# Hardware loops for half of the weighted sums over V in a two-problem decode attention kernel

## The chip, the cores and the metric

The kernel runs on one core of a Trainium2 chip. A core has TensorE (PE: matrix products, with a separate queue PEld for loading the stationary operand), VectorE (DVE), ScalarE (ACT), GpSimd (POOL) and SyncE (SP), and 16 DMA engines that bring data from HBM into the on-chip memory. The metric is the device time of one execution in microseconds (us), the median of three runs. Lower is better.

## What is computed

Two independent problems, A and B, of the same shape are solved one after the other and their results are put side by side. Each is one decoding step of attention with a sliding window: two sequences, one query position, 32 query heads that share 16 key/value heads, a head size of 128, and the last 4096 of 16384 cached positions.

```python
W = min(4096, max(256, Sk // 4))                       # 4096
q = (x @ wq) ...                                       # 2 x 32 heads x 128
k, v = k_cache[:, :, Sk - W:, :], v_cache[:, :, Sk - W:, :]   # each shared by 2 query heads
p = softmax(q k^T * Dh ** -0.5)
o = p v
return o @ wo                                          # 2 x 1 x 576 per problem
```

Each key and value is used by two query heads only, so there is little arithmetic per byte: the caches alone are 134 MB, and the profile counts 153 MB read from HBM.

## The kernel before, in words

**Slabs.** The work is cut into 16 slabs, eight per problem: slab i belongs to group G = i // 2 (four key/value heads) and to sequence b = i % 2. A slab has one K part and one V part of 4 MB each. Both go through a ring of four buffers (`ring`, 32,768 bytes per partition each). SP issues all large transfers, in the order in which the list `stream` has them (K of slab t, then V of slab t - 3, with parts of the output weights `wob` after every four slabs), and waits before each until the last reader of the ring buffer has finished (line 373). The last reader of a K part is the second DVE transposition `X` (line 436), the last reader of a V part is the last matmul of `PV` (line 539).

**One step of the main loop** (lines 700 to 740) handles slab t. DVE transposes the first half of K (`X`, L436, 4.43 us each), PE multiplies it with the queries (`S`, 16 matmuls, recorded at L462 and, through a helper that reuses loaded weights, at L266), then the same for the second half. Between them stand DVE's evacuation of the sum over V from the step before (`evac`, L562 and L569) and, in turn, the maximum of a group (L470) or the turning of its probabilities (`pT`, L509). After the second half, PE does a small transposition (`bias`, L490) or sums (`sums`, L520, and `dg`, L576), and then the sum over V of slab t - 3.

**The sum over V** (`PV`, `pv_moving`, L528) has eight rounds of four matmuls. Each matmul takes 32 columns of the turned probabilities `pT` as stationary operand and 512 columns of the V part as moving operand; the four of a round use the four 32-column strips of the PE array and accumulate into four strips of the PSUM bank `OTB`. Every matmul brings its own weight load. All are written out: 32 matmuls and 32 loads per slab, 512 of each in all.

**P in memory.** `pT` holds, for each of two groups in turn, 2048 columns as [h][b][j][q] with h the half of K, b the sequence, j 64 positions and q eight rows, so that the columns of one sequence are two separate stretches.

**Order.** There is no scheduler: each engine runs its instructions in the order of the calls. A recorder (`_Sched`) derives the semaphore waits, and `emit` (L813) writes the streams out: SP, PE, DVE, ACT, POOL.

**The end.** After the last V part come the last pieces of the output weights of problem B (cut in lines 162 and 360), the products with them (`proj`), two evacuations to `out_w` and the output transfers (L694).

Of the kernel before, what the change touches and what calls it, by code (L numbers as in the profile page):

```python
# [63 lines left out]
def build_kernel(nc, probs, out):  # L64
# [17 lines left out]
    KJ = W // 32  # L82
    SW = KJ * 128
# [3 lines left out]
    NSLAB = NG * Bb  # L87
# [6 lines left out]
    with es:  # L94
        sb = lambda name, shape, dt: es.enter_context(nc.sbuf_tensor(name, shape, dt))
        ring = sb("ring", [128, NSLOT, SW], BF16)
# [3 lines left out]
        pR = sb("pR", [128, 2048], BF16)  # L100
        pT = sb("pT", [128, 2, 2048], BF16)
# [38 lines left out]
        OTB = ps("ot")  # L140
# [6 lines left out]
        ringf = ring[:].rearrange("p r f -> p (r f)")  # L147
# [32 lines left out]
        for P in range(NPROB):  # L180
            def f_wq(e, P=P):
# [7 lines left out]
        pe = lambda fn, deps, tag: S.add("pe", fn, deps, tag)  # L189
# [3 lines left out]
                                                   base=0, channel_multiplier=1), [p_ones_f], "ident_f")  # L193
        p_ones_b = pool(lambda e: e.memset(ones_b[:], 1.0), [], "ones_b")
        p_ident_b = pool(lambda e: e.affine_select(ident_b[:], ones_b[:], [[-1, 128]], ALU.is_equal, 0.0,
                                                   base=0, channel_multiplier=1), [p_ones_b], "ident_b")
# [126 lines left out]
        for t in range(NSLAB + LAG):  # L323
            if t < NSLAB:
                stream.append(("K", t))
            if t >= LAG:
                i = t - LAG
# [178 lines left out]
        def make_pT(G):  # L506
            v = G % 2
            deps = [exp_op[G]] + ([PVop[2 * (G - 2) + 1]] if G >= 2 else [qt_op])
            pT_op[G] = dve(lambda e: e.transpose(  # L509
                pT[:, v, :].rearrange("p (w j q) -> p j w q", w=4, q=8),  # L510
                pR[:].rearrange("p (j w q) -> p j w q", w=4, q=8)), deps, "pT%d" % G)

        def make_rsum(G):
            ch[(G, "rsum8")] = pool(lambda e: e.tensor_tensor(
# [13 lines left out]
        def pv_moving(i, j0, j1):  # L528
            G, b = i // 2, i % 2
            v = G % 2  # L530
            r = slot_of[("V", i)]

            def f(e):
                for rd in range(j0 // 16, j1 // 16):
                    jh, j = rd // 4, 16 * (rd % 4)
                    base = (2 * jh + b) * 512 + 8 * j
                    for c in range(4):
                        jj = 16 * rd + 4 * c
                        last = e.matmul(OTB[32 * c:32 * c + 32, :], pT[:, v, base + 32 * c:base + 32 * c + 32],  # L539
                                        ring[:, r, jj * 128:(jj + 4) * 128], start=rd == 0, stop=rd == KJ // 16 - 1, skip_group_check=True)  # L540
                return last
            return f

        def make_PV(i, ks=None):
            ensure(("V", i))
            G, b = i // 2, i % 2
            parts = stream_dma[("V", i)]
            for c0, c1, dma in parts if ks is None else [parts[k] for k in ks]:
                deps = [dma, pT_op[G], evac_op[i - 1] if i >= 1 else q_ev[0]]
                PVop[i] = pe(pv_moving(i, c0, c1), deps, "PV%d_%d" % (i, c0))  # L550
            last_reader[("V", i)] = PVop[i]
# [148 lines left out]
        for t in range(NSLAB):  # L700
            i = t - LAG
# [13 lines left out]
            if Gs is not None:  # L715
                make_rsum(Gs)
                make_pT(Gs)
# [23 lines left out]
        i = T - LAG  # L741
# [9 lines left out]
        make_pick(NG - 2)  # L751
        make_rsum(NG - 1)
        make_pT(NG - 1)
        make_sums(NG - 1)
        make_PV(i + 2)
# [57 lines left out]
        def emit(eng_name, engine):  # L813
            for op in S.ops[eng_name]:
                for s_h, val in waits_of[id(op)]:
                    engine.wait_ge(s_h, val)
                last = op.fn(engine)
                if op.shared is not None:
                    last.then_inc(op.shared, 1)
                elif op.dma is None:  # L820
                    last.then_inc(ev[eng_name], 1)

        emit("sp", nc.sync)
        nc.sync.wait_ge(out_sem, dma_count[out_sem])
        emit("pe", nc.tensor)
        emit("dve", nc.vector)
        emit("act", nc.scalar)
        emit("pool", nc.gpsimd)


def bass_concat_heads__sliding_block_cached__sliding_block_cached__decode_kernel(
    nc, A_x, A_k_cache, A_v_cache, A_wq, A_wo, B_x, B_k_cache, B_v_cache, B_wq, B_wo, out,
):
    build_kernel(nc, [(A_x, A_k_cache, A_v_cache, A_wq, A_wo), (B_x, B_k_cache, B_v_cache, B_wq, B_wo)], out)
# [28 lines left out]
```

## Time and profile before

| what | value |
|---|---|
| time, median of 3 runs (lowest to highest) | 363.1 us (363.03 to 363.24) |
| time of the profiled execution | 363.1 us |
| its span, first to last instruction | 361.8 us |
| mean granted TensorE clock | 0.887 |
| data read from HBM | 153.1 MB, 423 GB/s over the span |
| busy: PE, DVE, ACT, POOL | 63%, 60%, 13%, 7% |
| PE instructions recorded | 1357 matmuls, 943 weight loads |
| sums over V (L539) | 512 matmuls, 32.0 us busy; 512 loads, 12.4 us busy |

The page of the profile has numbered parts: busy time by engine, the span in 40 slices, the DMA queues, the chain of work that ended last, the costliest groups of instructions (busy us, mean ns of one, idle time before them and what ended it), and the DMA issues. Other views are the timeline of a stretch, the busy time in chosen windows, one source line with its instructions, and who waited for whom. `SPq`, `PEldq` and the like are the engines' sequencers. `q8 instruction` is a DMA queue that brings instructions.

### The profile page before, as it was taken

The page shows a single profiled execution, that of the slowest core. Times are in us where ns is not written, and L with a number is a line of the kernel's source. Part 1 is how long each engine was busy: PE and PEld are TensorE (multiplying, and loading weights), DVE is VectorE, ACT ScalarE, POOL GpSimd, SP SyncE. Part 2 cuts the span into 40 slices and gives each one's busy share as a digit, 9 for nine tenths or more (in the row PEclk, how much of TensorE's full clock was granted, in tenths as well). Part 3 has the DMA queues.
Part 4 walks back from the last instruction along what each step waited for, and adds up shares of the span by engine and source line. Part 5 has one row for each costly group of instructions (what it writes and reads, how often), then busy time and mean ns, then how long its engine had stood idle before and what let it go on. Part 6 is the DMA issues. An engine that isn't in the chain of part 4 may idle for free.

```text
span 361.8 us, 2701 instructions
## 1 busy us (share of the span) xinstructions
PE 229.0 (63%) x1357; PEld 56.1 (16%) x943; DVE 218.6 (60%) x150; ACT 45.4 (13%) x77; POOL 24.3 (7%) x84
## 2 busy tenths in 40 slices
PE   0397687767464866671696656662776675667575
PEld 0010111112110211120121211110112121112222
DVE  0811898495949392924919493952927776675522
ACT  1002100040031002200005000500005000500500
POOL 4200101100010001000010000000010000001000
PEclk9999698969999889888798998899589897869989
DMA  8999999999999999999999999999999999999996
GB/s 327 449 428 420 442 426 424 446 413 446 417 447 420 442 422 422 439 438 420 438 424 434 431 438 412 448 420 442 424 435 429 428 438 420 434 442 420 427 417 258
DMA packets 6088, 153.28 MB, mean 424 GB/s; under 512 B 684, under 2 KB 828, under 8 KB 1084
## 3 DMA queue, kind: packets, MB, share of 16 engines
q1 hardware_dynamic: 6056, 153.10, 98.7%
q8 instruction: 9, 0.15, 0.2%
q14 instruction: 3, 0.02, 0.0%
q10 hardware_dynamic: 20, 0.01, 0.0%
HBM read 153.10 MB, written 0.00 MB: 423 GB/s over the span
## 4 chain that ended last, share of the span: by engine, by line
DMA 49%; DVE 24%; PE 16%; issue 8%; ACT 1%; POOL 1%; SPq 0%
DMA ring<-in_B_k_cache_dram 25%; DVE xt L436 15%; DMA ring<-in_B_v_cache_dram 9%; DMA ring<-in_B_wq_dram 7%; DMA ring<-in_A_k_cache_dram 6%; PE st L266 6%; PE st L462 5%; DMA wob<-in_B_wo_dram 3%; DVE oR L569 2%; DVE mx L470 2%; DVE pT L509 2%; PE pj L266 2%; DVE tmp L562 2%; PE ot L539 1%; ACT pR L500 1%
## 5 line engine op out<-in xcount | busy, mean ns | idle before, releaser
L462 PE MATMUL st<-xt,zq 128*128 128x512 bf16 x256 | 119.3, 466 | 93.6 <-DVE xt L436 93.6
L436 DVE STREAM_TRANSPOSE xt<-ring 128x4096 f32<-128x4096 f32 x32 | 141.6, 4429 | 33.5 <-DMA ring<-in_A_k_cache_dram 18.2
L266 PE MATMUL st<-xt,zq 128*128 128x512 bf16 x256 | 118.0, 461 | 0.0
L500 ACT ACTIVATE pR<-st,bias 128x512 bf16<-128x512 f32 x32 | 40.0, 1419 | 219.0 <-DVE bias L493 219.0
L462 PEld LDWEIGHTS st<-xt,zq 128*128 128x128 bf16 x256 | 28.3, 110 | 211.5 <-DVE xt L436 110.0
L539 PE MATMUL ot<-ring,pT 128*32 128x512 bf16 x512 | 32.0, 393 | 8.3 <-DMA ring<-in_B_v_cache_dram 8.3
L493 DVE SCALAR_TENSOR_TENSOR bias<-vmask,tb,offm 128x4 f32<-128x4 f32 x8 | 1.8, 224 | 37.1 <-PE tb L490 37.1
L523 DVE TENSOR_REDUCE ssum<-tb 128x2 f32<-128x8 f32 x8 | 1.3, 162 | 33.4 <-PE tb L520 33.4
L428 POOL TENSOR_TENSOR zq<-qs,bmask 128x64 bf16<-128x64 bf16 x32 | 8.6, 292 | 161.2 <-PE st L266 140.3
L509 DVE STREAM_TRANSPOSE pT<-pR 128x2048 bf16<-128x2048 bf16 x8 | 18.4, 2303 | 0.7 <-ACT pR L500 0.7
L562 DVE SCALAR_TENSOR_TENSOR tmp<-ot,rsb,dmask 128x512 f32<-128x512 f32 x16 | 11.5, 719 | 9.4 <-PE ot L539 9.4
L281 PE MATMUL ot<-ring,pT 128*32 128x512 bf16 x18 | 7.6, 421 | 15.1 <-DMA ring<-in_A_wq_dram 14.5
L539 PEld LDWEIGHTS ot<-ring,pT 128*32 128x32 bf16 x512 | 12.4, 99 | 23.7 <-DMA ring<-in_B_v_cache_dram 10.5
L569 DVE TENSOR_REDUCE oR<-tmp 128x128 f32<-128x512 f32 x15 | 15.6, 1039 | 0.5
L266 PE MATMUL pj<-ring,pT 128*32 128x512 bf16 x36 | 12.1, 422 | 0.0
L266 PE MATMUL pj<-wob,oM 128*2 128x288 bf16 (+1 forms) x64 | 10.2, 256 | 0.0
L470 DVE TENSOR_REDUCE mx<-st 128x2 f32<-128x1024 f32 x8 | 9.7, 1208 | 0.1
L500 ACT ACTIVATION_READ_ACCUMULATOR pR<-st,bias 128x1 f32 x32 | 9.1, 283 | 0.0
L636 PE MATMUL pj<-wob,oM 128*2 128x288 bf16 x32 | 7.9, 286 | 0.0
L224 DVE TENSOR_TENSOR xt<-xt,hmask 4x1152 bf16<-4x1152 bf16 x2 | 2.8, 1398 | 8.4 <-DMA xt<-in_A_x_dram 8.4
L266 PE MATMUL st<-ring,pT 128*32 128x512 bf16 x18 | 7.4, 414 | 0.0
L472 POOL TENSOR_TENSOR mv<-mx,v 128x2 f32<-128x2 f32 x8 | 1.6, 195 | 80.0 <-DVE mx L470 80.0
(71 smaller groups left out, 79.5 us busy)
## 6 DMA issues: line engine op xcount, KB each, us to landing
ring<-in_A_k_cache_dram SPq DMA_DIRECT2D x8, 4096.0 KB, 24.9
ring<-in_A_v_cache_dram SPq DMA_DIRECT2D x8, 4096.0 KB, 30.0
ring<-in_B_k_cache_dram SPq DMA_DIRECT2D x8, 4096.0 KB, 28.5
ring<-in_B_v_cache_dram SPq DMA_DIRECT2D x7, 4096.0 KB, 31.8
ring<-in_A_wq_dram SPq DMA_DIRECT2D x1, 4608.0 KB, 13.6
ring<-in_B_wq_dram SPq DMA_DIRECT2D x1, 4608.0 KB, 24.1
wob<-in_A_wo_dram SPq DMA_DIRECT2D x2, 2304.0 KB, 29.8
ring<-in_B_v_cache_dram SPq DMA_DIRECT2D x1, 2560.0 KB, 26.9
```

Source lines behind the costliest of these rows:

```text
L266: return e.add_instruction(mybir.InstMatmult(name=nc.get_next_instruction_name(), engine=mybir.EngineType.PE, ins=[e.lower_ap(mv_), e.lowe ...
L281: last = e.matmul(QB[c], wt, mv_, start=first, stop=True, skip_group_check=True)
L428: last = e.tensor_tensor(dst, src, msk, ALU.mult)
L436: Xop[(t, jh)] = dve(lambda e: e.transpose(xt[:, jh, :].bitcast(FP32).rearrange("p (kp x kt) -> p x kp kt", kp=2, kt=2), ring[:, r, jh * H ...
L462: last = e.matmul(ob, wt, mv_, start=first, stop=True, skip_group_check=True)
L470: ch[(G, "max")] = dve(lambda e: e.tensor_reduce(mx[:], st[:, :].rearrange("p (x t) -> p t x", t=2), AX.X, ALU.max), [Sop[(2 * G + 1, 1)]] ...
L500: last = e.activation(pR[:].rearrange("p (x k) -> p k x", k=4)[:, kv, :], st[:, :].rearrange("p (x t) -> p t x", t=2)[:, kv % 2, :], ACTF.Exp,
L509: pT_op[G] = dve(lambda e: e.transpose(pT[:, v, :].rearrange("p (w j q) -> p j w q", w=4, q=8), pR[:].rearrange("p (j w q) -> p j w q", w= ...
L539: last = e.matmul(OTB[32 * c:32 * c + 32, :], pT[:, v, base + 32 * c:base + 32 * c + 32], ring[:, r, jj * 128:(jj + 4) * 128], start=rd == ...
L562: evac_op[i] = dve(lambda e: e.scalar_tensor_tensor(tv, o, rsb[:, v, b:b + 1], dm, ALU.mult, ALU.mult), deps, "ev%d" % i)
L569: ch[(G, "red%d" % b)] = dve(lambda e: e.tensor_reduce(oR[:, b, :], tmp[:].rearrange("p (j d) -> p d j", j=4), AX.X, ALU.add), [evac_op[i] ...
L636: last = e.matmul(PJ[0], oM[:, j, :], mv_, start=start and j == 0, stop=True, skip_group_check=True)
```

## The change

For the eight slabs of problem A (`i < NSLAB // 2`) the rounds 1 to 6 of the sum over V become a loop of the PE sequencer, `e.Fori(1, 7)`, between a written-out round 0 and a written-out round 7. In the loop the addresses of the probabilities and of the V part come from registers: each round runs the loop body of four matmuls with their loads, five instructions that compute addresses in registers (26 register operations together), one addition to the counter and one compare-and-branch. The slabs of problem B stay written out. Matmuls executed are the same; 160 matmuls with their 160 loads leave the PE program text, and 72 register, branch and counter instructions come in.

So that one address step serves all eight rounds, `pT` is now ordered [b][h][j][q]: the columns of a sequence are one stretch of 1024. The DVE transposition that writes it gets one more dimension in its output pattern; its size stays 128 x 2048. PE's stream is now written out last, since a loop splits the program into stretches.

```diff
             pT_op[G] = dve(lambda e: e.transpose(
-                pT[:, v, :].rearrange("p (w j q) -> p j w q", w=4, q=8),
-                pR[:].rearrange("p (j w q) -> p j w q", w=4, q=8)), deps, "pT%d" % G)
+                pT[:, v, :].rearrange("p (b h j q) -> p j h b q", b=2, h=2, q=8),
+                pR[:].rearrange("p (j h b q) -> p j h b q", b=2, h=2, q=8)), deps, "pT%d" % G)
...
+            def one(e, wt_at, mv_at, first):
+                for c in range(4):
+                    wt, mv_ = pT[:, v, bass.ds(wt_at + 32 * c, 32)], ringf[:, bass.ds(mv_at + 512 * c, 512)]
+                    last = e.add_instruction(mybir.InstMatmult(
+                        name=nc.get_next_instruction_name(), engine=mybir.EngineType.PE,
+                        ins=[e.lower_ap(mv_), e.lower_ap(wt, for_matmul_weights=True)], outs=[e.lower_ap(OTB[32 * c:32 * c + 32, :])],
+                        start_tensor_calc=first, stop_tensor_calc=True, bass_skip_group_check=True,
+                        tile_size=(128, 32), tile_position=(0, 32 * c)))
+                return last
+
             def f(e):
+                if i < NSLAB // 2:
+                    one(e, b * 1024, r * SW, True)
+                    with e.Fori(1, 7) as rd:
+                        one(e, rd * 128 + b * 1024, rd * 2048 + r * SW, False)
+                    return one(e, b * 1024 + 7 * 128, r * SW + 7 * 2048, False)
                 for rd in range(j0 // 16, j1 // 16):
-                    jh, j = rd // 4, 16 * (rd % 4)
-                    base = (2 * jh + b) * 512 + 8 * j
-                    for c in range(4):
-                        jj = 16 * rd + 4 * c
-                        last = e.matmul(OTB[32 * c:32 * c + 32, :], pT[:, v, base + 32 * c:base + 32 * c + 32],
-                                        ring[:, r, jj * 128:(jj + 4) * 128], start=rd == 0, stop=rd == KJ // 16 - 1, skip_group_check=True)
+                    last = one(e, b * 1024 + rd * 128, r * SW + rd * 2048, rd == 0)
                 return last
...
         emit("sp", nc.sync)
         nc.sync.wait_ge(out_sem, dma_count[out_sem])
-        emit("pe", nc.tensor)
         emit("dve", nc.vector)
         emit("act", nc.scalar)
         emit("pool", nc.gpsimd)
+        emit("pe", nc.tensor)
```

## The prediction, made before the result was known

> **What bounds the kernel now.** I read the slices and the DMA queues first, then the chain that ended last, then the timeline of two steps in problem A, then how far SP's issues run ahead, and last the instruction queue.
>
> Page, parts 2 to 5 (slices of 9.0 us; queues as packets, MB, share of 16 engines; chain; two groups):
>
> ```profile
> PEclk9999698969999889888798998899589897869989
> DMA  8999999999999999999999999999999999999996
> ...
> q1 hardware_dynamic: 6056, 153.10, 98.7%
> q8 instruction: 9, 0.15, 0.2%
> ...
> DMA 49%; DVE 24%; PE 16%; issue 8%; ACT 1%; POOL 1%; SPq 0%
> ...
> L539 PE MATMUL ot<-ring,pT 128*32 128x512 bf16 x512 | 32.0, 393 | 8.3 <-DMA ring<-in_B_v_cache_dram 8.3
> L509 DVE STREAM_TRANSPOSE pT<-pR 128x2048 bf16<-128x2048 bf16 x8 | 18.4, 2303 | 0.7 <-ACT pR L500 0.7
> ```
>
> The DMA engines are full from start to end: data packets alone take 98.7% of all sixteen. So the kernel ends when 153 MB have come in, plus a short tail. The last step of the chain in order of time says the same:
>
> ```profile
> 348.51 10.90 DMA wob<-in_B_wo_dram
> ```
>
> From 348.51 + 10.90 = 359.41 us to the end of the span are 2.4 us of products and output, which this change does not touch. PE's work in problem A counts only if it lets the DMA queue run dry.
>
> Timeline of two steps (start, us, engine, line; in brackets the idle time before):
>
> ```profile
> 104.70 1.91 PE L539 MATMUL ot<-ring,pT 128*32 128x512 bf16 x32
> ...
> 106.66 0.54 SPq L380 DMA_DIRECT2D ring<-in_A_v_cache_dram  x1
> ...
> 109.45 0.41 PE L462 MATMUL st<-xt,zq 128*128 128x512 bf16 x1 [2.84 <-DVE xt L436]
> ...
> 124.20 1.91 PE L539 MATMUL ot<-ring,pT 128*32 128x512 bf16 x32
> ...
> 128.23 0.41 PE L462 MATMUL st<-xt,zq 128*128 128x512 bf16 x1 [2.12 <-DVE xt L436]
> ```
>
> A sum over V takes 1.91 us for 64 instructions, 30 ns each. After it PE idles 2.84 or 2.12 us until DVE has turned the next K half. SP, which waits for the last of these matmuls, issues the next transfer at once; queued behind that wait are all later transfers.
>
> **How much lateness the queue takes.** The source line of the ring transfers gives, from issue to landing:
>
> ```profile
> DMA to landing us min/median/max: 19.9/30.3/34.1
> ```
>
> 4.19 MB at 430 GB/s take 9.75 us, so an issue comes at least 19.9 - 9.75 = 10.1 us before the queue would be dry. Beside that, the compute round is shorter than the DMA round: the first X of slabs 4 and 6 start at 87.65 and 123.73, so two steps take 36.1 us; the DMA needs 4 x 9.75 for them plus 2.7 for its share of `wob` (2304 KB, 5.5 us every four slabs), 41.7 us. Spare per two slabs: 5.6 us.
>
> **The change part by part.**
>
> *The six looped rounds.* Let a round cost the sequencer r. Rows: PE's sequencer takes 51 ns for a semaphore instruction (the twelve at L816: 51/51/51); a tensor instruction passes in 30 ns. Lower bound: seven control instructions (five address steps, addition, branch) at 51 ns and eight tensor instructions at 30 ns, 0.60 us. Upper bound: the longest sequencer row, SP's 535 ns per DMA issue, for each of the seven, 3.99 us. The five address steps hold 26 register operations; if each operation costs one 51 ns row, 28 x 51 + 240 ns = 1.7 us. I take 1.7, since that row is of the same sequencer. Dispatch of the loop is then 10.2 us per slab, against 6 x 0.24 = 1.43 us of execution.
>
> Whether this shows depends on how far the sequencer runs ahead of PE. The instruction queue tells. Its nine packets of 16 KB for 2300 recorded instructions are 64 bytes each, 256 instructions per packet. The windows (PE and PEld busy, counts in brackets) ended at the second and the seventh packet:
>
> ```profile
> 0.00:108.30 108.30, 68.15 (x310) 13.23 (x176) 64.21 (x39) 12.96 (x24) 12.57 (x41) 0.92 0.99 423
> ...
> 0.00:308.65 308.65, 195.09 (x1006) 44.81 (x683) 190.94 (x118) 35.15 (x60) 23.00 (x79) 0.89 1.00 428
> ```
>
> 486 and 1689 instructions had started, 26 and 103 short of 2 x 256 and 7 x 256. If packets are fetched as the sequencer crosses a page, its lead over PE varies by 77 instructions and so reaches at least that many in places: more than the 64 of a whole sum over V. Then the loop is dispatched while PE still works on, or waits for, the K products before it: from 92.14 (first K matmul of the step) to 104.70 are 12.6 us, in the next step 109.45 to 124.20, 14.7 us; both exceed 10.2. Total dispatch per step, 10.2 plus some 76 written instructions at 30 ns, is 12.5 us of 18 to 21. So PV should start and end where it did: cost 0. Without this cover the sum would grow by e = 10.2 - 1.43 = 8.8 us per slab; that is a rival.
>
> A jump back needs its page of instructions still there; every page so far was brought once (nine packets for nine pages), and no row shows a return. [...]
>
> *pT.* Its output pattern gains a dimension. The K transposition already writes one with as many and takes 4429 ns for 4096 elements, 1.08 ns each, against 1.12 for pT: 2.2 us if it goes at that rate, 4.6 if writes halve. I take the 2.3 of now; even 4.6 adds 2.3 per two slabs, inside the spare 5.6. It has no gain to give, because DVE is not the bound.
>
> *The shorter program.* 320 instructions go, 72 come: 248, one packet of 256. A packet holds its DMA engine for 1.10 us (2.3% of 16 engines in the 3 us from 53 to 56). Nine on one engine would need 0.987 x 361.8 + 9.9 = 367 us, more than the span, so they are spread. Gain: 0 if other engines end as late, 1.1 if the one relieved was alone last. Seven or eight packets stay on others, so nearly 0; spread over sixteen, 0.07 us, which I take.
>
> *Problem B and the order of writing.* Same instructions at the same 97 ns per load and 379 ns per matmul; only the columns differ. The other engines' streams keep their order; the loops cut the program into 17 stretches, and if every stream passes a mark per new stretch, SP pays 16 x 17 ns (its semaphore row) = 0.3 us at the end, PE's 51 ns row would make it 0.8. I take 0.
>
> Sum: the profiled execution (363.1 us, span 361.8, 1.3 around it; it equals the median) + 0 - 0.07 + 0 + 0 = 363.0 us.
>
> **The rivals.**
>
> *Sequencer too slow (slower).* PV grows by e, of which 2.84 + 2.12 per two slabs is idle PE and 5.6 is spare. Lateness after four pairs is 4 x (2e - 4.96 - 5.6) = 8e - 42.2; past 10.1 us the queue runs dry, so it decides from e = 6.5. Without run-ahead e = 8.8: 28 - 10 = 18 us, 381 us. For it: no row shows a loop or a register address on PE, and a branch may empty what was queued. Against: the lead worked out above. With run-ahead it needs 6r + 2.3 above the mean 20.8 us of a step, r above 3.1.
>
> *A loop across a page (slower).* If one loop lies across two 16 KB pages and each jump back brings a page again, five returns wait for a fetch each: 1.10 us plus, say, two data packets ahead of it, 1.2 us each (in the 3 us from 53 to 56, 52 packets take 92.4% of 48 us, and 16 of them are tiny): 3.5 us, 17.5 in all, once. 2.8 are idle PE, 10.1 the least lead of the queue, so up to 4.7 us of dry queue; none at the median lead of 20.5. The further packets put a second 1.10 us on some engines. Price 1.1 to 5.8; nearer the median lead, 1.5: 364.5 us. For it: eight loops and eight page ends. Against: a body has 15 of 256 instructions, so a given loop straddles with 6%, one of eight with some 40%, and the neighbouring page may still be there.
>
> *The relieved engine was the last (faster).* -1.1 us, 362.0. Against: at least seven packets remain, each on some engine.
>
> **How the numbers follow.** No change 0.60. Sequencer 0.12, page 0.10, marks and other small costs over the bound 0.06: slower 0.28. Faster 0.12. Within 0.2% is 0.7 us, about what a measurement of this kernel can tell from no change. The range 362.2 to 366.0 takes in most of the faster rival's gain and most of the page rival; it leaves out the sequencer rival (0.12), the top of the page rival and the edge of the faster one, less than 0.2 together.
>
> **What would show it.** Right: q1 still near 98.7%; q8 with eight packets; L536 (the sums) in problem A again about 1.9 us from first to last; the K matmuls after them waiting for DVE, not for "issue"; issue to landing still near 30 us; pT at 2.3 us. Wrong: PE waiting for "issue" inside the sums, transfers landing less than 10 us after issue, DMA slices below 9, or more than nine packets on q8.

## The result, and the profile after

| | before | after |
|---|---|---|
| time, median (lowest to highest) | 363.11 us, 6 runs (363.03 to 363.34) | 364.95 us, 6 runs (363.56 to 371.78) |
| profiled execution: time, span | 363.1, 361.8 us | 363.56, 362.3 us |
| mean granted clock of it | 0.887 | 0.892 |
| ratio after / before | | 1.0045, 95% interval 1.0034 to 1.0056 |

The change costs 0.3 to 0.6%, where I forecast none. Four of its sixteen runs, one here and three in its second series, took 370.0 to 372.2 us at a granted clock of 0.866 to 0.875 and are not in the ratios, while no run of the kernel before took more than 363.5 us. The profiled execution is the quickest of the six, so the trace shows less of the loss than the median; the change was run and profiled a second time (span 363.7 us) to have a slower one.

Page of the kernel after, parts 2 to 5, the rows that answer those shown of before:

```profile
PEclk9999699969999698997989879898889888789969
DMA  8999999999999999999999999999999999999995
...
q1 hardware_dynamic: 6056, 153.10, 98.5%
q8 instruction: 8, 0.13, 0.1%
...
DVE 40%; PE 39%; DMA 9%; issue 7%; ACT 3%; POOL 1%; SPq 0%; DVEq 0%
...
L536 PE MATMUL ot<-ring,pT 128*32 128x512 bf16 (+1 forms) x512 | 57.4, 398 | 11.1 <-issue 9.3
L509 DVE STREAM_TRANSPOSE pT<-pR 128x2048 bf16<-128x2048 bf16 x8 | 18.4, 2302 | 1.2 <-ACT pR L500 1.2
```

The DMA engines are as full as before, one instruction packet fewer comes, and `pT` costs what it did. What changed is the chain that ended last: DMA had 49% of it and has 9%, DVE and PE now make up 79%. The sums over V went from 32.0 to 57.4 us busy, and PE now waits for "issue" in them.

Timeline of the sum over V in one step after (the kernel before has one row of 1.91 us there), from the matmul ahead of it to the K product behind it:

```profile
103.60 0.22 PE L490 MATMUL tb<-ident_f,nMrep 1*128 1x1 f32 x1 [1.28 <-POOL nMrep L486]
103.75 1.04 PE L536 MATMUL ot<-ring,pT 128*32 128x512 bf16 x8
105.05 0.88 PE L536 MATMUL ot<-ring,pT 128*32 x4 [0.26 <-issue]
106.19 0.85 PE L536 MATMUL ot<-ring,pT 128*32 x4 [0.26 <-issue]
107.32 0.85 PE L536 MATMUL ot<-ring,pT 128*32 x4 [0.28 <-issue]
108.43 0.89 PE L536 MATMUL ot<-ring,pT 128*32 x4 [0.26 <-issue]
109.58 1.15 PE L536 MATMUL ot<-ring,pT 128*32 x8 [0.26 <-issue]
110.66 0.41 PE L462 MATMUL st<-xt,zq 128*128 128x512 bf16 x1
```

Each looped round takes 1.13 us (105.05, 106.19, 107.32, 108.43) where a written one takes 0.24. The whole sum takes 6.9 us (103.75 to 110.66) where it took 1.91: e = 5.0 us. From first to last matmul six of the eight looped sums take 6.4 to 7.2 us, those of slabs 0 and 5 4.2 and 4.8. The K product behind it, which waited 2 to 3 us for DVE before, now starts without a wait.

PE's sequencer, by source line (count, then duration in ns, minimum/median/maximum): the address steps, the counter's instructions and the branch.

```profile
L538 PEldq FUSED_REGOPS  x192: 42/74/79, 82.6 to 243.3; - x192
...
L546 PEldq FUSED_REGOPS  x48: 78/78/83, 82.5 to 242.7; - x48
L546 PEldq ALU_OP  x48: 36/36/42, 83.5 to 243.5; - x48
L546 PEldq COMPARE_BRANCH  x48: 83/220/353, 83.6 to 243.6; - x48
```

A round is four address steps at 74, one at 78, the addition at 36 and the branch at 220 ns, 0.63 us; eight tensor instructions at 30 ns make 0.87; the 0.26 left stand in no row. Of the 48 branches, those that jump back measure 215 to 353 ns (median 220), and the last of each loop 83.

The lead of the transfers over the queue, by the source line of the ring transfers, after:

```profile
DMA to landing us min/median/max: 16.6/22.6/33.3
```

It was 19.9/30.3/34.1. Steps with loops became longer than the DMA needs (44.3 and 44.7 us per pair, against 41.7 by the sum in the prediction). From the trace, the end of the last data packet of a slab's K part, the start of the first K transposition of five slabs, and of the sum over V of slab 14 (us):

| | slab 8 | 10 | 12 | 14 | 15 | sum of slab 14 | this execution |
|---|---|---|---|---|---|---|---|
| last packet of K, before | 167.7 | 206.6 | 250.9 | 289.8 | 309.2 | | |
| before | 168.2 | 207.0 | 251.4 | 291.5 | 310.9 | 344.4 | 363.1 |
| after | 170.0 | 214.7 | 259.0 | 299.1 | 317.6 | 347.2 | 363.56 |
| after, second trace | 171.1 | 215.8 | 260.0 | 298.6 | 317.8 | 348.7 | 365.0 |

Before, slabs 8, 10 and 12 start 0.4 to 0.5 us after their last packet, and within 0.03 us of the landing that releases DVE: PE and DVE wait for the DMA there. After, PE and DVE are 8 us behind the data at slab 10. The last looped sum, of slab 7, runs in the step of slab 10, and yet they never catch up: against the kernel before they are 7.7 us late at slab 10, 6.7 at slab 15 and 2.8 at the sum of slab 14. The end shows what that does. The chain that ended last, its end in order of time (start, us, engine, tile, line), after:

```profile
344.75 2.31 DVE pT L509
347.21 3.60 PE ot L536 x32
351.77 0.54 PE st L392
...
353.20 1.19 PE ot L536 x20
...
355.67 0.79 PE ot L536 x12
```

No transfer stands in this end. The weights for which PE waited last in the kernel before land at 359.52 instead of 359.41, but PE is now still at products that it should have done earlier (output of the last evacuation issued at 361.00 instead of 360.46).

### The profile page after: what moved, and what is told of

It reads as the page before. It is cut to its first block, busy times and chain, and to the rows that moved or that the text cites. A ratio compares the mean times of both kernels' runs of the same rounds, so it can differ in the third digit from the quotient of the medians.

```text
span 362.3 us, 3045 instructions
## 1 busy us (share of the span) xinstructions
PE 251.5 (69%) x1357; PEld 67.5 (19%) x943; DVE 219.0 (60%) x150; ACT 45.4 (13%) x77; POOL 24.4 (7%) x84
## 3 DMA queue, kind: packets, MB, share of 16 engines
q1 hardware_dynamic: 6056, 153.10, 98.5%
## 4 chain that ended last, share of the span: by engine, by line
DVE 40%; PE 39%; DMA 9%; issue 7%; ACT 3%; POOL 1%; SPq 0%; DVEq 0%
DVE xt L436 24%; PE ot L536 12%; PE st L462 11%; PE st L266 11%; DMA ring<-in_A_k_cache_dram 9%; DVE pT L509 5%; DVE oR L579 4%; DVE tmp L572 3%; ACT pR L500 3%; DVE mx L470 2%; PE pj L266 2%; PE pj L646 1%; PE tb L586 1%; DVE oM L616 1%; POOL zq L428 1%
## 5 line engine op out<-in xcount | busy, mean ns | idle before, releaser
L462 PE MATMUL st<-xt,zq 128*128 128x512 bf16 x256 | 118.1, 461 | 65.9 <-DVE xt L436 65.9
L266 PE MATMUL st<-xt,zq 128*128 128x512 bf16 x256 | 116.6, 455 | 0.0
L536 PE MATMUL ot<-ring,pT 128*32 128x512 bf16 (+1 forms) x512 | 57.4, 398 | 11.1 <-issue 9.3
L536 PEld LDWEIGHTS ot<-ring,pT 128*32 128x32 bf16 (+1 forms) x512 | 23.7, 97 | 42.1 <-issue 28.8
L509 DVE STREAM_TRANSPOSE pT<-pR 128x2048 bf16<-128x2048 bf16 x8 | 18.4, 2302 | 1.2 <-ACT pR L500 1.2
L281 PE MATMUL ot<-ring,pT 128*32 128x512 bf16 x18 | 7.5, 414 | 15.7 <-DMA ring<-in_A_wq_dram 14.5
L281 PEld LDWEIGHTS ot<-ring,pT 128*32 128x32 bf16 x18 | 1.9, 103 | 30.3 <-DMA ring<-in_A_wq_dram 14.5
## 6 DMA issues: line engine op xcount, KB each, us to landing
wob<-in_A_wo_dram SPq DMA_DIRECT2D x2, 2304.0 KB, 25.8
```

The costliest lines, as they stand in the source:

```text
L266: return e.add_instruction(mybir.InstMatmult(name=nc.get_next_instruction_name(), engine=mybir.EngineType.PE, ins=[e.lower_ap(mv_), e.lowe ...
L281: last = e.matmul(QB[c], wt, mv_, start=first, stop=True, skip_group_check=True)
L462: last = e.matmul(ob, wt, mv_, start=first, stop=True, skip_group_check=True)
L509: pT_op[G] = dve(lambda e: e.transpose(pT[:, v, :].rearrange("p (b h j q) -> p j h b q", b=2, h=2, q=8), pR[:].rearrange("p (j h b q) -> p ...
L536: last = e.add_instruction(mybir.InstMatmult(name=nc.get_next_instruction_name(), engine=mybir.EngineType.PE, ins=[e.lower_ap(mv_), e.lowe ...
```

## Experiments

Each ran beside the kernel before, on one chip per group; ratios are to that kernel, with 95% intervals. My theory after the result: a loop's instructions are not run ahead, so most looped sums are some 5 us longer, and the lateness adds up until the end is late. Rivals: the new order of P or the 17 program stretches cost something; each loop or jump has a fixed price; the instruction packets fall elsewhere.

### Parts of the change

**No loops.** Only the order of P, the new form of the matmuls and PE's place in the program are kept (`if i < 0:` in place of `if i < NSLAB // 2:`).

> No loops at all: P ordered by batch and PE's stream written last, as in the change, but every sum over V written out. Theory lateness (the loops make each sum over V 6.9 us instead of 1.9, compute falls behind the DMA, and the end is late): 363.1 us, sums of 1.9 us, issue to landing of V near 30 us. Rival layout (the new order of P or of the streams costs it): 364.7 us as with the change. Rival fixed price (each loop costs some 0.2 us wherever it stands, 1.6 us for eight): 363.1 us.

Measured: 363.03 us (362.95 to 363.51), ratio 1.0001 [0.9992, 1.0010]; sums 1.9 us. The new order costs nothing: the loops make the loss.

**Loops in the first four slabs, and in the last four of problem A.**

```diff
-                if i < NSLAB // 2:
+                if i < 4:            # other kernel: 4 <= i < 8
```

> Loops in slabs 0 to 3 only. Lateness: half the delay is built up, some 9 us, less than the lead of the DMA queue, and twelve steps remain to make it good: 363.1 to 363.3 us; issue to landing falls to about 20 us around slab 5 and is near 30 us again in problem B. Fixed price: 0.8 us, 363.9 us.

> Loops in slabs 4 to 7 only, the same number as in slabs 0 to 3 but later. Lateness: the same 9 us of delay with eight steps to make it good: 363.1 to 363.6 us, not under the kernel with loops in slabs 0 to 3. Fixed price: 363.9 us, the same as there.

Measured: 363.00 us, ratio 0.9997 [0.9988, 1.0006], and 363.10 us, 1.0001 [0.9992, 1.0010]. Issue to landing has a median of 24.7 and 25.8 us. Half of the loops, in either half, cost nothing: no fixed price per loop of 1.6 / 8 us, which would give 0.8 us for four. Lateness at slab 14, against the kernel before, is 2.3 and 1.4 us, and the sum of slab 14 starts at 344.4 and 344.5 as before.

**Loops in slabs 0 to 14.**

```diff
-                if i < NSLAB // 2:
+                if i < NSLAB - 1:
```

> Loops in slabs 0 to 14. Lateness: the lead of the DMA queue is used up by about slab 9; from there the DMA waits for compute, steps of some 22 us against 20.8 us of DMA, and nothing is made good before the end: 370 to 376 us, DMA slices below 9 in the second half, issue to landing down to some 10 to 12 us. Fixed price: 15 x 0.2 = 3 us, 366.1 us.

Measured: 386.59 us (385.73 to 389.44), ratio 1.0668 [1.0630, 1.0707], more than I expected. Page of this kernel, slices and main queue:

```profile
DMA  8999999999999999999999999999996999999303
...
q1 hardware_dynamic: 6056, 153.10, 93.4%
```

The queue is idle for 6.6% of 385.0 us, 25.4 us against 1.3% of 361.8, 4.7 us, before. These 20.7 us are most of the loss of 23.2 us in the profiled execution. The loops in the last slabs stand between the last sums, where nothing else is left to do: the sum of slab 14 starts at 367.3, 22.9 us later than before, and the pieces of the last weights, which wait for the sums, are issued at 362.2 and 374.9 (before: 337.5 and 348.1), when the queue has been empty for 4.8 and 7.9 us. My sum had counted lateness per step only.

**Three iterations of two rounds each** (all eight slabs; half the jumps, same matmuls).

```diff
-                    with e.Fori(1, 7) as rd:
-                        one(e, rd * 128 + b * 1024, rd * 2048 + r * SW, False)
+                    with e.Fori(0, 3) as rd:
+                        one(e, rd * 256 + (b * 1024 + 128), rd * 4096 + (r * SW + 2048), False)
+                        one(e, rd * 256 + (b * 1024 + 256), rd * 4096 + (r * SW + 4096), False)
```

> The loops of problem A run three times over two rounds each: half the branches and counter steps, the same address steps and matmuls. A round's share of branch and counter is some 0.35 us in the trace of the change, so a sum over V takes about 5.9 us instead of 6.9. Lateness: about 1 us less per step, 8 us less in all: 363.2 to 363.9 us. Fixed price per loop: 364.7 us, as with the change.

Measured: 362.96 us, ratio 0.9998 [0.9989, 1.0007], faster than I expected, as the sums are shorter: six of the eight take 5.0 to 5.6 us from first to last matmul. Timeline, one sum (slab 1):

```profile
106.34 1.66 PE L536 MATMUL ot<-ring,pT 128*32 128x512 bf16 x12
108.31 1.46 PE L536 MATMUL ot<-ring,pT 128*32 x8 [0.31 <-issue]
110.04 1.76 PE L536 MATMUL ot<-ring,pT 128*32 x12 [0.27 <-issue]
```

An iteration of eight matmuls takes 1.73 us against 2 x 1.13. Some 1.4 us less per sum are enough to make all eight loops free: slab 14 starts at 294.3 (lateness 2.8), the sum of slab 14 at 344.3. The price is not in having loops, but in their length, past a point. The 17 program stretches are in this kernel too, so they cost nothing either.

### Why the sequencer does not run ahead

In the trace of the change the loop's first register instruction (a move into the counter) runs at 103.609 us. The bias product of L490, the last instruction before it that waits for a semaphore, starts at 103.601; in the next step the move runs at 125.656, 11 ns behind the start of the product of L586. In the two traces of the change the moves of six slabs come 6 to 12 ns after the start of the waiting product, which is 51 to 55 ns after its semaphore. Only in slabs 0 and 5, where the last waiting instruction is released 2 to 4 us before the sum, does the loop start early (slab 0: move at 82.39 with the K products at 82.31, sum from 86.3), and these sums take 4 to 5 us. So register instructions and branches seem held until every earlier instruction has its semaphore, even though the written matmuls of round 0 lie queued and each starts 3 to 4 ns after the one before.

**The sum ahead of the waiting product**, in the even steps: the sum over V is written before the small transposition (L490) that waits for POOL.

```diff
+            early = Gc is not None and 0 <= i < NSLAB // 2
+            if early:
+                make_PV(i)
...
-            if i >= 0:
+            if i >= 0 and not early:
```

> In the even steps of problem A the sum over V (with its loop, as in the change) stands before the small transposition that waits for POOL, not behind it. If the register instructions of the loop are held until every instruction before them has its semaphore (which is how the trace of the change reads), the first of them now starts when the second half of the K products is released, some 5 us before the sum, and the loop is dispatched while those products run: sums of even steps 3 to 4.5 us long instead of 6.9, those of odd steps 6 to 6.9 as before. If register instructions wait until PE is idle, all stay at 6 to 6.9 us. The time itself tells little: the transposition, and the next K transposition behind it, come later; 364 to 369 us.

Measured: 366.81 us (two runs), ratio 1.0103 [1.0078, 1.0129]. Timeline, the sum of the same slab as in the timeline after the change, above:

```profile
102.87 0.40 PE L266 MATMUL st<-xt,zq 128*128 128x512 bf16 x1
103.20 1.67 PE L536 MATMUL ot<-ring,pT 128*32 128x512 bf16 x20
105.12 0.85 PE L536 MATMUL ot<-ring,pT 128*32 x4 [0.26 <-issue]
106.27 1.13 PE L536 MATMUL ot<-ring,pT 128*32 x8 [0.30 <-issue]
107.33 0.22 PE L490 MATMUL tb<-ident_f,nMrep 1*128 1x1 f32 x1
```

With no waiting instruction between, five rounds are queued while the K products run: 20 matmuls without a gap, and the sum takes 4.2 us instead of 6.9. The sums of slabs 1, 3 and 7 take 4.2 to 4.3 us; those of slabs 2, 4 and 6, whose order was left alone, stay at 6.5 to 6.6, and slab 5, whose loop had started early already, gains nothing (5.4). That shows the mechanism in these kernels: what lies between a loop and its run-ahead is an unmet semaphore of an earlier instruction. The loop did not wait until that instruction was complete: in the trace of the change the move runs 8 ns after the start of a product that takes 0.22 us. The kernel as a whole is slower for another reason: the bias product, for which the next group's exponentials wait, comes at 107.33 instead of 103.60.

### A price that looked like that of the branches

**Empty loops.** The sums are written out, and an empty loop of six rounds stands ahead of each sum of problem A.

```diff
-                if i < NSLAB // 2:
+                if i < 8:
+                    with e.Fori(1, 7):
+                        pass
+                if i < 0:
```

> All sums over V are written out; before each of those of problem A stands a loop of six empty rounds (counter and branch only). The sum starts and ends some 2.0 us later, less than the 2.1 to 2.8 us that PE idles after it in the kernel before. Lateness: 363.1 to 363.3 us. Fixed price of a loop, or a branch that empties the queue at a cost not seen in the rows: 364 us or more.

Measured: 364.28 us (364.18 to 364.46), ratio 1.0034 [1.0021, 1.0047]: by what I had written, a price of the loops. But the steps are hardly late (slab 14 at 292.1, median from issue to landing 29.7). The end of its chain, and the product that waits last:

```profile
349.17 11.48 DMA wob<-in_B_wo_dram
360.69 0.23 PE pj L627 x2
```

These weights land at 360.65 us instead of 359.41. This kernel's PE program has 2356 instructions, 40 more than before, so its ninth instruction packet comes earlier, at 358.27 instead of 359.16, where in the kernel before it delayed nothing that PE awaited. Either the packet or the loops could be the cause; the two kernels with added matmuls, below, tell them apart.

**The change once more** (no edit), for a second trace and more runs.

> The changed kernel once more, beside the others on one chip, for a second trace: 364.7 us on the middle, 363.6 to 365.8 from run to run; the sum over V of slabs 1 to 7 at 6 to 6.9 us, issue to landing down to 16 to 18 us; where the time is above 364 us, either the DMA queue ran dry, or the last data came no later and the products behind it did.

Measured: 365.35 us (ten runs), ratio 1.0039 [1.0021, 1.0057]. Three runs with a granted clock of 0.892 took 363.35 to 363.73 us and four with 0.883 to 0.888 took 364.93 to 365.92; the first series has the same two groups (363.56 at 0.892; 364.61 to 365.71 at 0.887 to 0.888). The kernel without loops took 362.95 to 363.51 at any clock from 0.854 to 0.887. So with PE on the path that ends last, time and clock went together in these runs; that the clock is the cause was not tested.

**40 more instructions and no loop.** The kernel before, with 20 small matmuls at the start, where PE waits for its first weights.

```diff
+        def f_pad(e):
+            for _ in range(20):
+                last = e.matmul(STT[0][:, 0:128], ones_b[:, :], ones_b[:, :], start=True, stop=True, skip_group_check=True)
+            return last
+        pe(f_pad, [p_ones_b], "pad")
```

> The kernel before with 20 small matmuls (40 instructions with their weight loads) at the very start, while the tensor engine waits for its first weights; no loops. Its stream on the tensor engine has 2356 instructions, as many as that of the empty loops. If the price of the empty loops (1.2 us) is the ninth instruction packet, which came 40 instructions earlier and delayed the engine that still had the last piece of the output weights to bring, this kernel pays it too: 364.3 us, last landing of the output weights near 360.6. If the price comes from the branches and register instructions themselves: 363.1 us.

Measured: 364.22 us (364.17 to 364.67, 7 runs), ratio 1.0031 [1.0020, 1.0042]. The end of its chain:

```profile
348.71 11.93 DMA wob<-in_B_wo_dram
360.69 0.23 PE pj L620 x2
```

The same price without a loop, as forecast for the packet: the branches are not needed to explain it. The ninth packet came at 357.74, held its DMA engine 1.09 us, and the awaited weights landed at 360.64.

**Empty loops with 60 matmuls at the start**, so that the ninth packet comes earlier still (`range(60)`).

> The empty loops, with 60 small matmuls (120 instructions) more at the start, so that the ninth instruction packet comes some microseconds earlier, while the queue has data left for every engine to even it out. If the packet's place is the price: 363.1 to 363.3 us, last landing near 359.3 to 359.6. If the branches are: 364.3 us.

Measured: 364.33 us (364.19 to 364.53), ratio 1.0033 [1.0020, 1.0046], which I had written down for the branches. The packet came earlier, at 348.27, but the price stayed, so my idea that an early packet is evened out was wrong; the traces show that the packet made the price here too. Timelines of this kernel and of the kernel before, the sum over the first piece of the last V part:

```profile
351.83 1.26 PE L542 MATMUL ot<-ring,pT 128*32 128x512 bf16 x20 [1.30 <-DMA ring<-in_B_v_cache_dram]
```

```profile
350.51 1.26 PE L539 MATMUL ot<-ring,pT 128*32 128x512 bf16 x20 [1.45 <-DMA ring<-in_B_v_cache_dram]
```

By its packets the piece was in on 15 engines by 350.19 and on the last, right behind the instruction packet, at 351.35 (before: on all by 350.00), so PE was 1.3 us later, and the awaited weights landed at 360.71. With four loops (the kernel of the first four slabs) a packet at 347.98 did no such harm: it fell on an engine that was ahead, and the piece was in by 349.97. So in these kernels a packet cost 1.1 to 1.3 us where it fell on an engine that was already among the last; what decides the engine, these traces do not show.

### How the lateness adds up

**Loops in slabs 0 to 5** (`if i < 6:`).

> Loops in slabs 0 to 5, sums written out in the others. If the lateness of the tensor engine adds up over the slabs until it passes what the queue and the tail can take (four loops cost nothing, eight cost 1.6 us): 363.1 to 363.4 us, with a median from issue to landing between 22.6 and 24.7 us. If each loop has a fixed price, or having the loops beyond slab 3 at all: 364.3 us.

Measured: 363.14 us median, but 362.87 to 364.95 over 12 runs, ratio 1.0008 [0.9996, 1.0020]; median from issue to landing 21.7 us, below the 22.6 to 24.7 I gave. At slab 14 it is 3.4 us late, and its sum of slab 14 starts at 346.2. Within the measurement it is as fast as before, with single runs that are not: the eight runs at a clock of 0.886 to 0.892 took 362.87 to 363.26 us, the four at 0.878 to 0.883 took 363.41 to 364.95. No kernel of this study beats the one before: those with fewer or shorter loops only equal it.

**Eight loops, spread out**, in slabs 0, 1, 2, 4, 6, 8, 10 and 12.

```diff
-                if i < NSLAB // 2:
+                if i in (0, 1, 2, 4, 6, 8, 10, 12):
```

> Eight loops, as many as in the change, but in slabs 0, 1, 2, 4, 6, 8, 10 and 12, so that a step with a written-out sum lies between most of them and the tensor engine can catch up. If the price is lateness that adds up over consecutive slabs: 363.1 to 363.4 us. If it goes by the number of loops: 364.7 us. If it goes by how little time is left between the last loop and the end: between the two.

Measured: 370.36 us (six runs, 366.83 to 372.83), ratio 1.0211 [1.0174, 1.0248]: outside all that I had written. As many loops as in the change cost some four times as much, so the number is not what counts, and written sums in between don't undo the lateness either. Slab 12 starts 0.5 us late (251.9), slab 14 4.2 us and slab 15 6.0 us, and then the looped sum of slab 12 stands among the last sums, where no wait is left to hide in. Timeline of its end:

```profile
334.52 0.61 PE L536 MATMUL ot<-ring,pT 128*32 128x512 bf16 x8
...
339.74 1.11 PE L536 MATMUL ot<-ring,pT 128*32 x8 [0.28 <-issue]
342.29 1.91 PE L536 MATMUL ot<-ring,pT 128*32 128x512 bf16 x32
350.88 3.61 PE L536 MATMUL ot<-ring,pT 128*32 128x512 bf16 x32 [1.55 <-DVE ssum L523]
```

The executions with a trace now give one rule for this kernel. From the start of the sum of slab 14 to the end of the execution pass 16.35 us (change, 347.21 to 363.56), 16.3 (its second trace, 348.72 to 365.0), 16.2 (sums ahead of the waiting product, 351.74 to 367.98) and 15.95 (spread loops, 350.88 to 366.83): there PE's work sets the end. With an earlier start it is more: 17.2 (six loops, 346.19 to 363.41) and 18.7 (before, 344.41 to 363.1), since the last weights set it. So the kernel can take 363.1 - 16.3 - 344.4 = 2.4 us of lateness there, and beyond that each microsecond is a microsecond, as long as the queue does not run dry (with 15 loops it did, and 19.0 us pass). That holds for profiled executions; why the runs of the spread loops reach up to 372.8 us is not explained, because their mean clocks (0.894 to 0.899) do not tell them apart.

## Why the prediction was wrong, step by step

- **The six looped rounds, run-ahead: this step failed.** I took the fetching of instruction packets, which was 26 and 103 instructions ahead of PE, for a lead of dispatch, and so set the cost at 0. The traces show no such lead for these loops: the written matmuls of round 0 are queued and start 3 to 4 ns apart, but in six of the eight slabs the loop's first register instruction came only 51 to 55 ns after the semaphore of the product just ahead of it, and there the loop ran in full view. The prediction's own sign of being wrong, PE waiting for "issue" inside the sums, is what the profile shows.
- **r.** Taken as 1.7 us, bounds 0.60 and 3.99; measured 1.13. The error was to count 28 register operations at 51 ns; they are six instructions of 36 to 78 ns and a branch of 220. Without cover e is then 5.0 us (measured), not 8.8.
- **How much lateness the queue takes: this step failed too, and it made a loss possible at e = 5.0.** By the rival's own formula 2 x 5.0 - 4.96 - 5.6 = -0.6 us per pair, no lateness at all. The spare of 5.6 us came from one pair of steps (slabs 4 to 6, 36.1 us at a granted clock of 0.95). Later pairs without loops and without waiting took 40.1 us (before, slabs 12 to 14, clock 0.79; the change, same slabs, clock 0.87) and 42.2 (first four looped, slabs 8 to 10, clock 0.80, with 167 PE matmuls against 133), against 41.7 for the DMA: spare -0.5 to 1.6. With loops, pairs took 44.3 and 44.7, some 2.6 to 3.0 over the DMA.
- **What bounds the end.** I let the queue run dry be the only way to a loss, from 10.1 us of lateness. In the change it never did (q1 98.5%, awaited weights at 359.41 before and 359.52 after). The end became late through compute instead, from 2.4 us of lateness at the sum of slab 14, a path that the prediction did not have.
- **Sequencer too slow.** The rival was right in its mechanism (no run-ahead, waits for "issue" inside the sums), wrong in its price (381 us forecast, 364.95 measured) and in the point from which it decides (e = 6.5; taken at the sum of slab 1, nothing is lost with 5.4 us, e = 3.5, and 1.6 us with 6.9, e = 5.0, so the point lies between).
- **A loop across a page.** It gave 364.5, near the result, for a reason that was not seen: eight packets, none brought twice, and no branch above 353 ns, where the rival had returns of 3.5 us (its 17.5 - 2.8 - 10.1 is 4.6, not 4.7; nothing hangs on that). Whether a loop lay across a page end, no row shows. No row shows a jump back that brought a packet again either, so what one costs was not shown.
- **The shorter program, the relieved engine.** Eight packets, as forecast, and no gain from the one less that can be told: 0.9997 and 1.0001 in the kernels with four loops. Right as far as that goes, though incomplete: a packet on a late engine near the end cost 1.1 to 1.3 us.
- **pT, problem B, the order of writing.** 2302 ns for `pT`, as taken; the kernel without loops measures 1.0001, and that with two rounds per iteration, which has the 17 stretches, 0.9998. Right.

The range 362.2 to 366.0 held the time, but by luck: its upper part was there for the page rival, and the loss came from a rival that the range left out. The forecast of no change did not hold.

## What to carry to other kernels

A hardware loop on PE, in a stream full of semaphore waits, was not run ahead here: cost it at its full dispatch time (1.13 us per round of four matmuls with their loads) unless the last wait before it is met long before (2 to 4 us before the sum in slabs 0 and 5, whose sums took 4.2 and 4.8 us instead of 6.4 to 7.2). Measure the spare of a pipeline on steps late in the run, at the clock they get, and not on the first undisturbed pair; and ask beside "does the queue run dry" how late the last compute chain may start. Differences of 0.3% can come from where instruction packets fall, as the kernel with 40 more instructions shows (ratio 1.0031), so a kernel with the same number of instructions and without the suspect is a needed control.

## Not expected of the hardware

- The first register instruction of a loop on PE ran 6 to 12 ns after the start of the last earlier instruction that had to wait, in twelve of sixteen loops, and not before; with no wait unmet ahead of it, five rounds were queued (20 matmuls in 1.67 us without a gap).
- A taken compare-and-branch on PE's sequencer took 220 ns in the first trace and 212 in the second (medians of 48 with the exits; 83 and 76 at the least), an addition 36, an address step of several operations 42 to 83.
- A packet of 16 KB of instructions held its DMA engine 1.02 to 1.11 us in the kernel before. 20 small matmuls (40 instructions with their loads) at the start, where PE is idle, made the kernel 1.1 us slower, because the ninth packet met an engine that still had the last data to bring.
